# A gated sum of attention and a Fourier layer: the gate leaves VectorE's DFT updates for GpSimd's output stage

## The chip, the cores and the metric

The kernel runs on one core of a Trainium2 chip. A core has a matrix engine (TensorE, PE in the profile; its weight loads are listed as PEld), a vector engine (VectorE, DVE), a scalar engine (ScalarE, ACT), a general engine (GpSimd, POOL) and an engine that here only issues DMAs (SyncE, SP). Each engine executes its own instructions in order and waits on semaphores for the others. GpSimd also issues DMAs here, and these stand in its queue between its computations. The metric is the device time of one execution in microseconds (us), lower is better.

## The reference, cut to what matters

All matrices are f32. `x` is 2048 by 640. The two heavy branches are attention with 32 heads of 20 columns, and a Fourier layer written as products with DFT matrices. A sigmoid gate, one number per row of `x`, mixes the two.

```python
x = A_x
g = sigmoid((x * gate_w).sum(-1, keepdims=True))     # one gate per row
a = attention(x, wqkv) @ wo                           # 32 heads of 20 columns, softmax
re = x @ dft_hid_re.T ; im = x @ dft_hid_im.T
b = dft_seq_re @ re - dft_seq_im @ im                 # real part of the 2-D DFT
return g * a + (1 - g) * b
```

The question of this case is where the factor `1 - g` is applied to `b`, and by which engine.

## The kernel before

**Stages.** First come the projections of `x` (queries, keys, values, and part of the product with the hidden-dimension DFT). Then comes one long loop of 1024 steps over the attention: in each step PE multiplies keys and queries twice, ACT takes the exponential, and PE also makes, 41 steps ahead, the scores whose row maximum VectorE takes (`s_mm`, line 151 for the matmul, line 153 for the maximum). Every fourth step ends a cycle: PE multiplies the exponentials with the values in one block of 16 matmuls (`av_step`, line 435). Between the attention's matmuls PE gets the DFT's matmuls as fillers (`fill`): first the rest of the hidden-dimension products (`hid_tile`), and from about 600 us on the products along the sequence (`dft_step`, line 510). Last comes an output stage of 16 row tiles, in which PE multiplies the attention's result with `wo`.

**PSUM buffers.** The scores and the exponentials' inputs share five PSUM tiles, taken in turn (`bank`). A score tile is free again when VectorE has taken its maximum, so PE can run only some tiles ahead of VectorE. The output stage takes its PSUM tiles from the same five.

**The DFT along the sequence.** It is a block method with seven products (`PRODUCTS`) over halves of the rows and columns, so that each product's result is added to, or subtracted from, one, two or three quarter blocks of the result `y`. One unit is one product for one tile of 128 rows: 16 steps of DFT matmuls, 56 units in all. GpSimd prepares both operands: it combines the DFT matrix halves (line 406), and splits each operand into a rounded value and a rest (lines 94 and 95; tiles `part` for the DFT matrix, `a` for the data). `part` has three buffers.

**The end of a unit.** PE's two partial sums lie in PSUM. ACT copies one into the SBUF tile `m` (line 529), VectorE adds the other (line 530). Then `finish_y` runs once for each target, 96 times in all: it multiplies `m` with `1 - g` (or with its negative, from two small tiles `ngate`), and either writes that into the target tile `yt` (line 544, the first time) or adds the target's earlier content, which was loaded from DRAM (line 542). Three steps later SP stores `yt` to the scratch `y_scr` in DRAM. `run_extras` calls these pieces at the end of every fourth step, so the VectorE instructions of `finish_y` stand in the stretch in which PE executes its block of 16 matmuls.

**The output stage.** SP loads whole rows of `y` (`load_y`, tiles of 128 by 640 in buffers of `p`) and of the attention's result (`load_o`), ACT and VectorE split the latter (`fins`), PE makes two halves of a row tile with 15 matmuls each, and VectorE forms `g * ps + y` (line 701) and so frees the PSUM tile. The last attention unit's normalisation is spread into the same stage: its pieces (`rest`) put DMAs and one multiplication into GpSimd's queue, and the attention rows from tile 8 on can only be loaded after it.

```python
for fn in rest[:2]:      # GpSimd: store_l (4 DMAs), load_l (1 DMA)
    fn()
fins[1]()
for tt in range(NS):
    ...                  # PE; VectorE line 701, twice
    for fn in {2: rest[2:5], 3: rest[5:6], 4: rest[6:]}.get(tt, ()):
        fn()             # tt 2: reciprocal (VectorE), store_r, load_r; 3: norm; 4: store_o
```

Of the kernel before, what the change touches and what calls it, by code (L numbers as in the profile page):

```python
# [10 lines left out]
F32 = mybir.dt.float32  # L11
R = mybir.dt.float32r
AF = mybir.ActivationFunctionType
ALU = mybir.AluOpType
# [4 lines left out]
P = 128  # L19
# [5 lines left out]
NS = S // P  # L25
# [30 lines left out]
def mix_kernel(ctx: ExitStack, tc: tile.TileContext, xa, wqk, wb, cdft, wo, out):  # L56
    nc = tc.nc
    pe, act, dve, pool, sp = nc.tensor, nc.scalar, nc.vector, nc.gpsimd, nc.sync
    ctx.enter_context(tc.manual_schedule())

    def pools(**kw):
        return ctx.enter_context(tc.tile_pool(**kw))

    const = pools(name="const", bufs=1)
# [20 lines left out]
        pool.memset(f32(t), 1.0)  # L85
    logit = const.tile([P, NS], F32, name="logit")
    gate = const.tile([P, NS], F32, name="gate")
    ngate = {g: const.tile([P, NS], F32, name=f"ngate{g + 1}") for g in (1, -1)}

    def split(dst1, dst2, src, e1, e2):  # L90
        if e1 is act:
# [5 lines left out]
    def three(ps, st1, st2, mv1, mv2, first, last):  # L97
        pe.matmul(ps, st1, mv1, start=first, stop=False)  # L98
        pe.matmul(ps, st1, mv2, start=False, stop=False)  # L99
        pe.matmul(ps, st2, mv1, start=False, stop=last)  # L100
# [3 lines left out]
    def bank():  # L104
        return ps_w.tile([P, 512], F32, name=f"ps{next(turn) % 5}")
# [31 lines left out]
    def at_step(i, fn):  # L137
        later.setdefault(i, []).append(fn)
# [100 lines left out]
    def flush(keep=0):  # L239
        while len(stores) > keep:  # L240
            sp.dma_start(*stores.pop(0))
# [118 lines left out]
    for n, c in enumerate(order):  # L360
        for t in range(4):
            m = 4 * n + t
# [12 lines left out]
    act.activation(gate, logit, AF.Exp, scale=-1.0)  # L375
    dve.tensor_scalar(gate, gate, 1.0, None, op0=ALU.add)
    dve.reciprocal(gate, gate)
    for g in (1, -1):
        dve.tensor_scalar(ngate[g], gate, float(-g), float(g), op0=ALU.mult, op1=ALU.add)


    at = {}
# [106 lines left out]
    def dft_step(g):  # L489
# [34 lines left out]
        if s == NS - 1:  # L524
            m = apool[0].tile([P, HE], F32, name="m", bufs=2)
            y0, y1 = yp[0][:, :HE], yp[1][:, :HE]

            def read():
                act.activation(m, y0, AF.Copy)
                dve.tensor_tensor(m, y1, m, op=ALU.add)  # L530

            extras.append((now[0], read))
            for out_, y in zip(PRODUCTS[n][2], outs.pop((n, t))):
                extras.append((now[0] + 1, functools.partial(finish_y, out_, t, m, y)))
        yield

    def finish_y(target, t, m, y):
        sg, th, hf = target
        tt = th * HT + t
        gs = ngate[sg][:, tt : tt + 1]  # L540
        if (tt, hf) in seen:
            dve.scalar_tensor_tensor(y, m, gs, y, op0=ALU.mult, op1=ALU.add)
        else:
            dve.tensor_scalar(y, m, gs, None, op0=ALU.mult)
        seen.add((tt, hf))
        at_step(now[0] + 3, functools.partial(sp.dma_start, y_scr[tt, :, hf * HE : (hf + 1) * HE], y))

# [26 lines left out]
    def load_o(tt):  # L574
        raw = raw_tile()[:, : ND * P].rearrange("p (d c) -> p d c", d=ND)
        sp.dma_start(raw, o_scr[:, tt * P : (tt + 1) * P].rearrange("(d p) c -> p d c", p=P))

        def finish():
            o = part_tile().rearrange("p z c -> p (z c)")[:, : 2 * ND * P].rearrange("p (z d c) -> p z d c", z=2, d=ND)
            split(o[:, 0], o[:, 1], raw, act, dve)  # L580
            ops[tt] = o

        return finish
# [33 lines left out]
    for i in range(total + 1):  # L617
# [50 lines left out]
        if total - 10 <= i < total - 4 and i % 2 == 0:  # L668
            tt = (i - total + 10) // 2
# [11 lines left out]
    ys = {}  # L681

    def load_y(tt):
        ys[tt] = pair_tile().rearrange("p z c -> p (z c)")[:, :D]
        sp.dma_start(ys[tt], y_scr[tt])

    flush()
    for tt in range(4):
        load_y(tt)
    for fn in rest[:2]:  # L690
        fn()
    fins[1]()
    for tt in range(NS):
        y, o = ys.pop(tt), ops.pop(tt)
        for hf in range(2):
            ps = bank()[:, :HE]
            for d in range(ND):
                w = wos[d, hf]
                three(ps, o[:, 0, d], o[:, 1, d], w[:, 0], w[:, 1], d == 0, d == ND - 1)
            ye = y[:, hf * HE : (hf + 1) * HE]  # L700
            dve.scalar_tensor_tensor(ye, ps, gate[:, tt : tt + 1], ye, op0=ALU.mult, op1=ALU.add)  # L701
        if 0 < tt < NS - 3:
            load_y(tt + 3)
        for fn in {2: rest[2:5], 3: rest[5:6], 4: rest[6:]}.get(tt, ()):
            fn()
        if tt + 3 < NS:
            fins[tt + 3] = load_o(tt + 3)
        sp.dma_start(out[tt * P : (tt + 1) * P, :], y)
        if tt + 2 < NS:
            fins[tt + 2]()  # L710


# [33 lines left out]
```

## Time and profile before

| | |
|---|---|
| median of 3 runs | 2012.11 us (2010.03 to 2013.65) |
| profiled execution, its own time | 2012.72 us |
| its span in the profile | 2011.0 us |
| mean granted PE clock in it | 0.997 of full speed |
| busy: PE, DVE, ACT, POOL | 98%, 75%, 62%, 49% of the span |

The span runs from the first to the last instruction; 1.7 us of the execution's own time lie around it. A busy share is an average over stages. PE's matmuls are pipelined and their ends are modelled, so that a short stall can be hidden in "busy". In the timeline, a number in brackets is the idle time of the engine ahead of the instruction, with what ended it.

### The profile page before, as it was taken

How to read it: one execution, taken by the hardware profiler on the slowest of the kernel's cores; microseconds unless marked ns; L12 is line 12 of the kernel's file. 1: busy time of each engine (PE TensorE's matmuls, PEld its weight loads, DVE VectorE, ACT ScalarE, POOL GpSimd, SP SyncE). 2: the span in 40 equal slices, each digit the busy share in tenths (PEclk: the TensorE clock that was granted, in tenths of full speed). 3: DMA queues.
4: the chain of work that ended last, by engine and by line, in shares of the span. 5: the costliest groups of instructions: out<-in, count | busy, mean ns of one | idle time of the engine just before them, and what ended most of it. 6: DMA issues, size and time to landing. Idle time of an engine off the chain costs nothing. (4 is left out here: it accounts for less than half of the span.)

```text
span 2011.0 us, 44080 instructions
## 1 busy us (share of the span) xinstructions
PE 1974.8 (98%) x17080; PEld 1397.7 (70%) x17080; DVE 1501.9 (75%) x2516; ACT 1253.3 (62%) x2337; POOL 986.6 (49%) x898
## 2 busy tenths in 40 slices
PE   8999999999999999999999999999999999999999
PEld 7987767666675666666666666666666666666679
DVE  3144568878887888888888888888888888888423
ACT  4221147777776666677666666766766676667751
POOL 1210001111006888556368876974775689576510
PEclk9999999999999999999999999999999999999999
DMA  6653321313125475435266736563555556444345
GB/s 218 168 166 132 128 90 45 83 50 82 35 60 161 143 204 159 118 100 153 93 169 194 207 133 194 175 184 100 165 149 145 163 171 200 131 149 144 95 150 184
DMA packets 196514, 281.05 MB, mean 140 GB/s; under 512 B 73372, under 2 KB 137916, under 8 KB 194384
## 3 DMA queue, kind: packets, MB, share of 16 engines
q1 hardware_dynamic: 158992, 246.20, 39.6%
q0 software_dynamic: 37312, 32.03, 6.4%
q8 instruction: 134, 2.20, 0.5%
q14 instruction: 76, 0.62, 0.1%
HBM read 213.81 MB, written 63.70 MB: 138 GB/s over the span
## 5 line engine op out<-in xcount | busy, mean ns | idle before, releaser
L153 DVE TENSOR_REDUCE mx<-ps 128x1 f32<-128x512 f32 x2048 | 1262.2, 683 | 233.8 <-PE ps L151 230.1
L641 ACT ACTIVATE p<-ps 128x512 f32<-128x512 f32 x2048 | 1122.6, 598 | 446.0 <-PE ps L151 354.6
L151 PE MATMUL ps<-kst,qst 60*128 60x512 f32 x2048 | 926.1, 460 | 8.0 <-ACT p L641 3.7
L638 PE MATMUL ps<-qst,kst 62*128 62x512 f32 x2048 | 823.9, 409 | 9.0 <-DVE mx L153 7.6
L510 PE MATMUL yp<-a,part 64*128 64x320 f32 x5376 | 734.0, 309 | 0.1
L510 PEld LDWEIGHTS yp<-a,part 64*128 64x128 f32 x5376 | 596.6, 187 | 23.9 <-DVE m L530 0.3
L638 PEld LDWEIGHTS ps<-qst,kst 62*128 62x128 f32 x2048 | 376.9, 185 | 235.9 <-DVE mx L153 66.9
L435 PE MATMUL av<-p,v 128*21 128x512 f32 x4096 | 494.7, 599 | 0.1
L151 PEld LDWEIGHTS ps<-kst,qst 60*128 60x128 f32 x2048 | 372.0, 184 | 59.5 <-ACT p L641 27.7
L95 POOL TENSOR_TENSOR part<-raw,part 128x1024 fp32r<-128x1024 f32 x112 | 267.1, 2385 | 9.0
L435 PEld LDWEIGHTS av<-p,v 128*21 128x21 f32 x4096 | 98.8, 100 | 226.8 <-issue 219.8
L287 PE MATMUL yp<-wb,xs 64*128 64x320 f32 x1920 | 238.1, 308 | 0.4 <-ACT raw L295 0.3
L94 POOL CAST part<-raw 128x1024 fp32r<-128x1024 f32 x112 | 116.8, 1043 | 205.2 <-PE yp L510 198.6
L406 POOL TENSOR_TENSOR raw<-raw,raw 128x1024 f32<-128x1024 f32 x78 | 188.3, 2414 | 50.1 <-DMA raw<-in_cdft 39.6
L287 PEld LDWEIGHTS yp<-wb,xs 64*128 64x128 f32 x1920 | 205.7, 187 | 9.1 <-ACT raw L295 0.6
L467 POOL TENSOR_TENSOR o<-o,rb 128x512 f32<-128x512 f32 x32 | 41.6, 1300 | 160.7 <-DMA rb<-r_scr 130.0
L94 POOL CAST wb<-raw 128x966 fp32r<-128x966 f32 (+1 forms) x4 | 3.4, 856 | 229.7 <-PE av L435 195.5
L95 POOL TENSOR_TENSOR a<-araw,a 128x320 fp32r<-128x320 f32 x112 | 98.1, 876 | 9.0
L95 DVE TENSOR_TENSOR p<-ps,p 128x512 fp32r<-128x512 f32 x40 | 27.5, 691 | 94.2 <-ACT p L92 94.2
L98 PE MATMUL ps<-xs,part 128*128 128x512 f32 x200 | 80.7, 403 | 9.1 <-ACT xs L92 7.5
L92 ACT ACTIVATE p<-ps 128x512 fp32r<-128x512 f32 x40 | 23.7, 597 | 101.5 <-PE ps L100 101.5
L420 POOL TENSOR_TENSOR araw<-araw 128x320 f32<-128x320 f32 x80 | 71.4, 892 | 20.4 <-DMA araw<-a_scr 19.9
(67 smaller groups left out, 1339.0 us busy)
## 6 DMA issues: line engine op xcount, KB each, us to landing
raw<-in_cdft SPq DMA_DIRECT2D x192, 512.0 KB
araw<-a_scr SPq DMA_DIRECT2D x192, 160.0 KB
qk_scr<-p SPq DMA_DIRECT2D x40, 512.0 KB
y_scr<-yt SPq DMA_DIRECT2D x96, 160.0 KB
kst<-qk_scr POOLq DMA_DIRECT2D x32, 320.0 KB, 12.2
qst<-qk_scr POOLq DMA_DIRECT2D x64, 160.0 KB, 8.8
a_scr<-raw SPq DMA_DIRECT2D x64, 160.0 KB
yt<-y_scr SPq DMA_DIRECT2D x64, 160.0 KB
```

The lines of the kernel that those rows point to most:

```text
L94: e1.tensor_copy(dst1, src)
L95: e2.tensor_tensor(dst2, src, f32(dst1), op=ALU.subtract)
L98: pe.matmul(ps, st1, mv1, start=first, stop=False)
L151: pe.matmul(ps, q[b : b + KROWS, qt * P : (qt + 1) * P], k[b : b + KROWS, kc * 512 : (kc + 1) * 512], start=True, stop=True)
L153: return lambda: dve.tensor_reduce(mx[n][:, h, qt, kc : kc + 1], ps, axis=AX.X, op=ALU.max)
L287: pe.matmul(yp[h][:, :HE], xs[r, xz, d, cs], w[r, wz, d, :HE], start=d == 0 and z == 0, stop=d == ND - 1 and z == 2)
L406: pool.tensor_tensor(raws[0], raws[0], raws[1], op=ALU.add if PRODUCTS[n][0][1][0] > 0 else ALU.subtract)
L420: pool.tensor_tensor(raws[0], raws[0], raws[1], op=ALU.add if PRODUCTS[n][1][1][0] > 0 else ALU.subtract)
L435: pe.matmul(av[32 * j : 32 * j + DH + 1, :], v[:, kt, h * (DH + 1) : (h + 1) * (DH + 1)], pp[qc][:, h, :], start=kt == 0, stop=kt == NS - 1)
L510: pe.matmul(yp[h][:, :HE], c[r, cz, cs], a[r, az], start=s == 0 and z == 0, stop=s == NS - 1 and z == 2)
L638: pe.matmul(pt, k[b : b + KROWS + 2, kt * P : (kt + 1) * P], q[b : b + KROWS + 2, qc * 512 : (qc + 1) * 512], start=True, stop=True)
L641: act.activation(pp[:, h], pt, AF.Exp, scale=float(DH) ** -0.5)
```

## The change

`finish_y` no longer multiplies with the gate and no longer runs on VectorE. GpSimd adds `m` to the target or subtracts it, or, the first time, writes `m` times plus or minus one. So `y_scr` holds `b` without its factor. In the output stage GpSimd multiplies each loaded row tile of `y`, 128 by 640, with `1 - g` in place (`scale_y`). Tiles 0 and 1 are multiplied ahead of the loop, tile `tt + 2` at the end of turn `tt`, so two turns ahead of its use. In GpSimd's queue the first multiplication stands directly behind `load_l`, those of tiles 2 and 3 before `store_r`, that of tile 4 between `load_r` and `norm`, that of tile 5 between `norm` and `store_o`, and the rest behind `store_o`. The order on PE, ACT and SP stays as it was.

```diff
-    ngate = {g: const.tile([P, NS], F32, name=f"ngate{g + 1}") for g in (1, -1)}
+    ngate = const.tile([P, NS], F32, name="ngate")
...
-    for g in (1, -1):
-        dve.tensor_scalar(ngate[g], gate, float(-g), float(g), op0=ALU.mult, op1=ALU.add)
+    dve.tensor_scalar(ngate, gate, -1.0, 1.0, op0=ALU.mult, op1=ALU.add)
...
     def finish_y(target, t, m, y):
         sg, th, hf = target
         tt = th * HT + t
-        gs = ngate[sg][:, tt : tt + 1]
         if (tt, hf) in seen:
-            dve.scalar_tensor_tensor(y, m, gs, y, op0=ALU.mult, op1=ALU.add)
+            pool.tensor_tensor(y, y, m, op=ALU.add if sg > 0 else ALU.subtract)
         else:
-            dve.tensor_scalar(y, m, gs, None, op0=ALU.mult)
+            pool.tensor_scalar(y, m, float(sg), None, op0=ALU.mult)
         seen.add((tt, hf))
...
+    def scale_y(tt):
+        pool.tensor_scalar(ys[tt], ys[tt], ngate[:, tt : tt + 1], None, op0=ALU.mult)
+
     flush()
     for tt in range(4):
         load_y(tt)
     for fn in rest[:2]:
         fn()
     fins[1]()
+    for tt in range(2):
+        scale_y(tt)
     for tt in range(NS):
...
         sp.dma_start(out[tt * P : (tt + 1) * P, :], y)
         if tt + 2 < NS:
+            scale_y(tt + 2)
             fins[tt + 2]()
```

## The prediction

> **What bounds the kernel now.** I read the page first, then the groups by line, then the stage of the DFT products alone, then single cycles in the timeline, and last the output stage. The page and the groups:
>
> ```profile
> span 2011.0 us, 44080 instructions
> PE 1974.8 (98%) x17080; PEld 1397.7 (70%) x17080; DVE 1501.9 (75%) x2516; ACT 1253.3 (62%) x2337; POOL 986.6 (49%) x898
> ...
> L638 PE MATMUL ps<-qst,kst 62*128 62x512 f32 x2048 | 823.9, 409 | 9.0 <-DVE mx L153 7.6 <-DVE p L95 0.7 <-ACT p L641 0.3
> ```
>
> PE is the bound; the other engines matter only where PE waits for them. The one wait with a DVE name on it is 7.6 us in front of line 638, ended by row maxima. The first row of the next fence is the stretch in which `finish_y` runs; its PE idle time is 1265.00 - 1256.75 = 8.25 us.
>
> ```profile
> 670.00:1935.00 1265.00, 1256.75 (x11534) 843.92 (x11532) 1039.44 (x1740) 884.82 (x1653) 870.36 (x742) 1.00 0.51 152
> 1060.00:1320.00 260.00, 255.76 (x2337) 171.85 (x2335) 225.50 (x369) 178.82 (x332) 212.41 (x182) 1.00 0.59 178
> ```
>
> The columns are length, then busy time and count of PE, PEld, DVE, ACT, POOL, then clock and DMA. More than half of the idle time, 260.00 - 255.76 = 4.24 us, lies in the 260 us in which POOL is 82% busy (212.41). Why there, three durations tell (min/median/max in ns, from the view of tile `m`), and one cycle in the timeline (start, duration):
>
> ```profile
> L542 DVE SCALAR_TENSOR_TENSOR yt<-m,ngate,yt x64: 529/550/2671, 865.2 to 1934.1; 128x320 f32<-128x320 f32 x64
> L530 DVE TENSOR_TENSOR m<-yp,m x56: 468/492/493, 673.8 to 1931.2; 128x320 f32<-128x320 f32 x56
> L544 DVE TENSOR_SCALAR yt<-m,ngate x32: 366/412/2531, 680.0 to 1210.9; 128x320 f32<-128x320 f32 x32
> ```
>
> ```profile
> 1306.72 0.14 PEld L435 LDWEIGHTS av<-p,v 128*21 128x21 f32 x8 [0.29 <-issue]
> 1307.47 3.65 DVE L542 SCALAR_TENSOR_TENSOR yt<-m,ngate,yt 128x320 f32<-128x320 f32 x2
> 1308.13 2.63 POOL L406 TENSOR_TENSOR raw<-raw,raw 128x1024 f32<-128x1024 f32 x1
> 1308.55 2.92 SPq L621 DMA_DIRECT2D y_scr<-yt  x2
> ...
> 1311.04 2.47 DVE L153 TENSOR_REDUCE mx<-ps 128x1 f32<-128x512 f32 x4
> 1311.77 0.50 PE L638 MATMUL ps<-qst,kst 62*128 62x512 f32 x1 [1.18 <-DVE mx L153]
> ...
> 1315.02 0.28 PE L179 MATMUL ps<-ident,nm 128*16 128x128 f32 x1
> 1315.22 0.14 PEld L435 LDWEIGHTS av<-p,v 128*21 128x21 f32 x8
> ```
>
> Two updates that take 0.55 us each when nothing is in their way took 3.65 us, and the second ended 0.36 us after a POOL instruction of 2.63 us (1308.13 + 2.63 = 1310.76; 1307.47 + 3.65 = 1311.12). Line 530, which has one operand in PSUM, never took over 493 ns beside the same POOL. So the updates, which read and write SBUF alone, are held by a running POOL instruction, the row maxima start late, the five PSUM tiles stay full, and PE stands 1.18 us. A cycle without that, between two starts of PE's block of 16, against 8.50 us above:
>
> ```profile
> 1005.58 0.14 PEld L435 LDWEIGHTS av<-p,v 128*21 128x21 f32 x8 [0.28 <-issue]
> 1012.18 0.14 PEld L435 LDWEIGHTS av<-p,v 128*21 128x21 f32 x8 [0.28 <-issue]
> ```
>
> That is 6.60 us with the same number of DFT fillers. The held cycle also has the small transpose of line 179 (0.28), so the hold cost 8.50 - 6.60 - 0.28 = 1.62 us where the idle column shows 1.18, 1.37 times as much.
>
> **The change part by part.** (1) *The updates leave DVE.* 96 instructions go, and with them the holds. Line 153 reads PSUM, and no other DVE instruction of this stage has two large SBUF operands. At least PE's 7.6 us named after DVE come back; at most the whole idle time, 8.25, times 1.37, so 11.3 us. I take the middle, 9.5. What is late next in a released cycle is PE itself, as in the 6.60 us cycle.
>
> (2) *The updates come to POOL*, 64 as an add of two tiles and 32 as a multiplication by a constant. The nearest rows are POOL's own, same tile size, and the larger forms:
>
> ```profile
> L95 POOL TENSOR_TENSOR a<-araw,a 128x320 fp32r<-128x320 f32 x112 | 98.1, 876 | 9.0
> L94 POOL CAST a<-araw 128x320 fp32r<-128x320 f32 x112 | 52.7, 471 | 25.4 <-DMA araw<-a_scr 20.3
> L467 POOL TENSOR_TENSOR o<-o,rb 128x512 f32<-128x512 f32 x32 | 41.6, 1300 | 160.7 <-DMA rb<-r_scr 130.0 <-ACT p L641 29.5 <-DMA yt<-y_scr 1.3
> L95 POOL TENSOR_TENSOR part<-raw,part 128x1024 fp32r<-128x1024 f32 x112 | 267.1, 2385 | 9.0
> L94 POOL CAST part<-raw 128x1024 fp32r<-128x1024 f32 x112 | 116.8, 1043 | 205.2 <-PE yp L510 198.6 <-PE ps L638 1.8 <-PE ps L151 1.4
> ```
>
> 64 x 0.88 + 32 x 0.47 = 71 us (87 us if the multiplication costs as much as an add). POOL has 1265.00 - 870.36 = 395 us free in the stretch. Each update now also waits in POOL's queue for line 530 of its unit; behind it stand the next splits of `part` and `a` for PE, and the DMAs that load `kst` and `qst`. What covers that is POOL's lead: the last row says that 198.6 of the 205.2 us that it stood before a split ended when PE gave back a `part` buffer, so POOL is normally early by most of a buffer's life. I take nothing for it; uncovered, it costs PE up to two updates, 1.8 us, a unit. SP's store of `yt`, three steps later, waits for POOL instead of DVE; in the held cycle above it waited 2.92 us for DVE, so SP loses nothing.
>
> (3) *The output stage gets 16 multiplications of 128 by 640 on POOL.* The trace has no such instruction. With one input, the casts (471 at 320 columns, 1043 at 1024) give 0.73 us; as costly as an add (1300 at 512, 2385 at 1024) it would be 1.57. I take 0.85, near the cast, as one tensor is read. What counts is its place:
>
> ```profile
> 1937.25 2.00 POOL L451 DMA_DIRECT2D l_scr<-o  x4 [28.85 <-ACT o L442]
> 1944.00 0.58 POOL L454 DMA_DIRECT2D lc<-l_scr  x1 [4.74 <-DVE p L701]
> ...
> 1961.49 1.31 POOL L467 TENSOR_TENSOR o<-o,rb 128x512 f32<-128x512 f32 x1 [4.62 <-DMA rb<-r_scr]
> 1963.10 2.04 POOL L475 DMA_DIRECT2D o_scr<-o  x4 [0.29 <-POOL o L467]
> ```
>
> ```profile
> 1936.27 0.35 PE ps L98
> ```
>
> ```profile
> 1938.71 0.55 DVE L701 SCALAR_TENSOR_TENSOR p<-ps,gate,p 128x320 f32<-128x320 f32 x1 [0.21 <-PE ps L100]
> 1940.91 0.55 DVE L701 SCALAR_TENSOR_TENSOR p<-ps,gate,p 128x320 f32<-128x320 f32 x1 [1.65 <-PE ps L100]
> 1941.38 0.81 DVE L95 TENSOR_TENSOR part<-raw,part 128x640 fp32r<-128x640 f32 x1
> ...
> 1969.86 0.83 DVE L95 TENSOR_TENSOR part<-raw,part 128x640 fp32r<-128x640 f32 x1 [2.00 <-ACT part L92]
> ```
>
> POOL issues its four stores at 1937.25 and then stands until 1944.00, when the load of what they wrote may go; the wait is put down to DVE, but it fits the stores' landing. The first multiplication is queued behind that load: 1944.58 + 0.85 = 1945.43, where line 701 for tile 0 ran at 1938.71. DVE waits there, and behind it stands the split of tile 2 (line 95, before at 1941.38). DVE now does line 701 twice (1945.50, 1945.97), arrives at the split at 1946.44, finds POOL in the multiplication of tile 2 until 1947.15, and is done at 1947.97. PE needs it in its third matmul for tile 2. Tiles take 4.40 us (two halves of 1940.91 - 1938.71 = 2.20), so tile 2 starts at 1936.27 + 8.80 = 1945.07, the third matmul 2 x 2.20 / 15 = 0.29 later, at 1945.36. **PE stands 2.6 us** here. The cheap end (0.73, no hold by POOL) gives 1.8, the dear one (1.57, held for one whole multiplication) 4.2. PSUM has room: tile 0's two halves are freed before the sixth half needs one.
>
> Further on, the whole chain shifts with PE, except that the multiplication of tile 4 stands before `norm` (hidden in its 4.62 us wait) and that of tile 5 before the store of `o`, which shifts by 0.85. The split of tile 8 ended at 1969.86 + 0.83 = 1970.69 and was due at 1936.27 + 8 x 4.40 + 0.29 = 1971.76: 1.07 us of room, enough for 0.85; at 1.57 plus a hold of 1.57 it would cost 2.1. Later multiplications have two turns, 8.8 us, and cost nothing.
>
> Here a rule speaks against the change. The split of the output stage took 0.81 us while POOL was idle. The Trainium skill, GPSIMD Engine Reference, § 1 Specifications, says that GpSimd's SBUF interfaces are shared with VectorE and that instructions with two SBUF inputs or in a 2-port mode contend. Lines 542 and 530 agree: 2671 against 493 ns at most. By this rule the splits of this stage, two SBUF inputs each, are open to holds for the first time, which is what the 0.71 us above is.
>
> **The sum.** -9.5 + 2.6 = -6.9 us. Against the profiled execution's own 2012.72 us that is 2005.8; that execution was 0.6 above the median of 2012.11, so the median after is **2005.2 us**. With the ends: -11.3 + 1.8 = -9.5, so 2002.6; and -7.6 + 4.2 + 2.1 = -1.3, so 2010.8. A difference under 0.2%, 4.0 us, can hardly be told from none here, so that the dear output stage would read as no change.
>
> **The rivals.** *A dear multiplication on POOL.* If a multiplication by a column of 128 numbers runs like an add or worse, the output stage gives back 5 to 9 us and the kernel stands at 2008.2 to 2012. For it: no such row in the trace. Against it: one tensor input, as in the cast.
>
> *PE does not gain.* Another wait takes the place of the holds, and only the output stage's price is left: 2012.1 + 2.6 = 2014.7, within 0.2%. Against it: the 7.6 us in the groups, and the undisturbed cycle of 6.60.
>
> *POOL becomes the bound, and the kernel is slower.* In 1060 to 1320 POOL has 260.00 - 212.41 = 47.6 us free. Line 530 ran 56 times between 673.8 and 1931.2, so a unit lasts 1257.4 / 55 = 22.9 us; with two targets each (all products but the last two) some 22 updates fall into these 260 us. From 47.6 / 22 = 2.2 us each, waits for line 530 included, POOL falls behind and PE waits for `part`. At 2.8 us each this costs 22 x 0.6 = 13 us: 2012.1 - 9.5 + 2.6 + 13 = 2018.2. For it: one update in POOL's strict order now holds back everything behind it until PE has finished a unit. Against it: 0.88 us, and POOL's lead. The Trainium skill, GPSIMD Engine Reference, § 4.1 Engine selection, advises against this: elementwise work on two inputs belongs on VectorE, as GpSimd is about twice as slow. The rows agree on the engine's time, 876 against 550 ns; by engine time alone the change would lose, but neither engine is the bound.
>
> **How the numbers follow.** Forecast (below 2008.1): 0.73. Dear multiplication: 0.10, and no gain: 0.06, both within 0.2%, so 0.16. POOL the bound, or a like starvation through the `qst` loads behind the updates: 0.11, slower. The range for 8 in 10 is the forecast's with its ends, 2002.6 to 2010.8, which takes in most of the dear case and leaves out about 0.2.
>
> **What would show it.** Right: no idle time of PE before line 638 ended by line 153 beyond about 1 us; cycles with an update as long as those without; PE idle time of 670 to 1935 under 2 us; the updates on POOL at about 0.9 and 0.5 us; in the output stage the first line 701 at about 7 us after its place before, and one PE stall of 2 to 3 us at tile 2. Wrong: PE waits for `part`, `a` or `qst`; a second stall at tile 8; multiplications over 1.6 us; or holds that remain without the updates.

## The result, and the profile after

| | median | range | ratio to before, 95% interval |
|---|---|---|---|
| before, same series | 2012.88 us | 2010.03 to 2014.97 | |
| changed kernel | **2001.86 us** | 2000.50 to 2004.27 | 0.995, 0.9936 to 0.9965 |
| changed kernel, second series | 2001.94 us | 1997.65 to 2004.88 | 0.9948, 0.993 to 0.9966 |
| changed kernel, third series | 2001.13 us | 1998.0 to 2004.21 | 0.9944, 0.993 to 0.9958 |

The kernel is faster by 0.5%, 11 us by the medians. The forecast was 6.9 us less, 2005.2 us; the measured median lies 0.7 us below the lower end of its range, 2002.6. Each ratio weighs the executions of both kernels in its own series, not the medians, and leaves out one of the kernel before in the second series, 2287.46 us at a granted clock of 0.753. The profiled execution took 2004.27 us, the slowest of its four, so that the two profiles differ by 8.5 us only; what follows compares stages, not ends. The page of the changed kernel, its group for line 636 (638 before), and the two stretches that were shown of before:

```profile
span 2002.5 us, 44148 instructions
...
PE 1972.5 (99%) x17080; PEld 1402.0 (70%) x17080; DVE 1428.3 (71%) x2419; ACT 1253.5 (63%) x2337; POOL 1096.9 (55%) x1010
...
L636 PE MATMUL ps<-qst,kst 62*128 62x512 f32 x2048 | 818.9, 407 | 2.1 <-DVE mx L153 0.9
```

```profile
670.00:1935.00 1265.00, 1261.83 (x11586) 853.29 (x11584) 966.57 (x1646) 885.67 (x1655) 956.38 (x845) 1.00 0.52 153
1060.00:1320.00 260.00, 259.58 (x2381) 174.58 (x2373) 207.07 (x353) 180.56 (x339) 231.91 (x205) 1.00 0.61 182
```

PE's wait for row maxima went from 7.6 to 0.9 us, and in 1060 to 1320 us, where POOL is now busy for 89% of the time, PE stands 0.42 us instead of 4.24. The first row also has PE's stall in the output stage in it, as that stage now begins 12 us earlier: 1.55 of its 3.17 us of idle time, which leaves 1.6. The cycle that was held before (8.50 us) looks like this now (timeline: start, duration):

```profile
1297.17 1.70 POOL L540 TENSOR_TENSOR yt<-yt,m 128x320 f32<-128x320 f32 x2
1298.24 0.14 PEld L434 LDWEIGHTS av<-p,v 128*21 128x21 f32 x8 [0.27 <-issue]
1299.08 1.14 SPq L619 DMA_DIRECT2D y_scr<-yt  x2
1300.65 2.49 DVE L153 TENSOR_REDUCE mx<-ps 128x1 f32<-128x512 f32 x4 [1.58 <-PE ps L151]
1305.03 0.14 PEld L434 LDWEIGHTS av<-p,v 128*21 128x21 f32 x8
```

From block to block it takes 1305.03 - 1298.24 = 6.79 us, 1.71 less. The two updates begin on POOL 1.07 us before the block and are done 0.63 us into it (1297.17 + 1.70 = 1298.87); VectorE waits for PE (1.58 us), no longer PE for VectorE; SP's stores take 1.14 us where they took 2.92. Over the whole stretch from the first update to the last regular cycle, the distances between these blocks add up to 1248.81 us against 1259.84, 11.0 less, nearly all of it gained in eleven of the cycles in which an update had been held. In the two other traces of the changed kernel they add up to 1248.51 and 1248.85 us.

POOL's new instructions (min/median/max in ns from the view by line, and the group of the output stage's multiplications):

```profile
L540 POOL TENSOR_TENSOR yt<-yt,m x64: 858/871/897, 855.7 to 1919.6; 128x320 f32<-128x320 f32 x64
L542 POOL TENSOR_SCALAR yt<-m x32: 998/1011/1038, 673.3 to 1198.1; 128x320 f32<-128x320 f32 x32
L686 POOL TENSOR_SCALAR p<-p,ngate 128x640 f32<-128x640 f32 x16 | 30.1, 1886 | 10.9 <-DMA p<-y_scr 8.1 <-DVE p L704 1.8 <-DVE part L95 0.8
```

The output stage, with line 704 in the place of 701:

```profile
1924.08 0.42 PE L98 MATMUL ps<-a,part 128*128 128x320 f32 x1
1930.71 0.57 POOL L453 DMA_DIRECT2D lc<-l_scr  x1 [3.58 <-DMA l_scr<-o]
1931.32 7.47 POOL L686 TENSOR_SCALAR p<-p,ngate 128x640 f32<-128x640 f32 x4
1933.25 1.01 DVE L704 SCALAR_TENSOR_TENSOR p<-ps,gate,p 128x320 f32<-128x320 f32 x2 [6.88 <-POOL p L686]
1934.18 0.81 DVE L95 TENSOR_TENSOR part<-raw,part 128x640 fp32r<-128x640 f32 x1
1935.05 0.42 PE L100 MATMUL ps<-a,part 128*128 128x320 f32 x1 [1.60 <-DVE part L95]
1961.87 0.41 PE L98 MATMUL ps<-a,part 128*128 128x320 f32 x1 [0.45 <-ACT part L92]
1962.73 0.42 PE L100 MATMUL ps<-a,part 128*128 128x320 f32 x1 [0.30 <-DVE part L95]
1997.94 0.55 DVE L704 SCALAR_TENSOR_TENSOR p<-ps,gate,p 128x320 f32<-128x320 f32 x1 [1.59 <-PE ps L100]
```

VectorE stands 6.88 us for the first scaled tile, PE then 1.60 us for the split of tile 2, and again around tile 8. The stage lasts 1998.49 - 1924.08 = 74.4 us, against 2007.46 - 1936.20 = 71.3 before (the first row of the next fence is from the timeline of the kernel before):

```profile
1936.20 0.42 PE L98 MATMUL ps<-a,part 128*128 128x320 f32 x1
...
2006.91 0.55 DVE L701 SCALAR_TENSOR_TENSOR p<-ps,gate,p 128x320 f32<-128x320 f32 x1 [1.65 <-PE ps L100]
```

So: 11.0 us gained in the DFT products, 3.2 lost in the output stage. This loss is not a fixed size: in the two other traces of the changed kernel the stage lasts 73.1 and 74.1 us, so that 1.9 and 2.8 are lost. The start of the loop and its first cycles, which the change doesn't touch, made up for most of the rest in this pair (first block 2.2 us earlier, the cycles until the first update 1.1 longer); up to the block ahead of the first update it took 672.8 us before, and 668.4, 671.7 and 673.1 us in the three traces of the changed kernel.

### The profile page after: what moved, and what is told of

Read it like the earlier page. It is cut to its first block, busy times and chain, and to the rows that moved or that the text cites. A ratio compares the mean times of both kernels' runs of the same rounds, so it can differ in the third digit from the quotient of the medians.

```text
span 2002.5 us, 44148 instructions
## 1 busy us (share of the span) xinstructions
PE 1972.5 (99%) x17080; PEld 1402.0 (70%) x17080; DVE 1428.3 (71%) x2419; ACT 1253.5 (63%) x2337; POOL 1096.9 (55%) x1010
## 5 line engine op out<-in xcount | busy, mean ns | idle before, releaser
L94 POOL CAST part<-raw 128x1024 fp32r<-128x1024 f32 x112 | 116.2, 1038 | 109.0 <-PE yp L509 104.4
L540 POOL TENSOR_TENSOR yt<-yt,m 128x320 f32<-128x320 f32 x64 | 55.1, 873 | 84.4 <-DVE m L529 82.4
```

The source lines that it names most:

```text
L94: e1.tensor_copy(dst1, src)
L540: pool.tensor_tensor(y, y, m, op=ALU.add if sg > 0 else ALU.subtract)
```

## The experiments

Theory 1 was the prediction's: VectorE's updates are held while POOL works, and the holds stall PE. Theory 2: VectorE simply had too much to do between PE's blocks. The first four runs tell these apart; three more take the output stage apart, and one puts the updates back on VectorE; the last two compare the best version once more.

**The changed kernel again.** 

> The changed kernel once more, as the base for the next three. Both theories: 2001.9 us, 0.995 of before. It also says how far the median of the changed kernel moves between series; the first series gave 2000.5 to 2004.3.

Measured: 2001.94 us, ratio 0.9948 (0.993 to 0.9966). It repeats.

**VectorE's time back, without a second SBUF input.**

```diff
             pool.tensor_scalar(y, m, float(sg), None, op0=ALU.mult)
+        dve.tensor_reduce(spare[:, :1], m, axis=AX.X, op=ALU.max)
```

> The changed kernel, and each of the 96 updates also puts one maximum over m (128 by 320, one SBUF input) into VectorE's queue at the place where the update was; its result is not used. Theory 1 (VectorE's updates cost time because an instruction with two SBUF inputs is held by a running GpSimd instruction): about 0.45 us each, 43 us more of VectorE, but no holds, so no change against the changed kernel, 2002 us, and PE's idle time ahead of line 636 ended by row maxima stays near 1 us. Theory 2 (VectorE simply had 83 us less to do in the stretches between PE's blocks): half of the gain or more is lost, 2007 us or above.

**The same place, with two SBUF inputs.**

```diff
             pool.tensor_scalar(y, m, float(sg), None, op0=ALU.mult)
+        dve.tensor_tensor(spare, m, m, op=ALU.add)
```

> As the run before, but the added VectorE instruction is an add of m and m into a spare tile (two SBUF inputs, 128 by 320), again unused. Theory 1: it is held like the updates were, up to 2.6 us, and most of the gain is lost, 2009 to 2013 us, with PE idle 5 to 8 us ahead of line 636. Theory 2: as long as the maximum, so the same time as that run, 2007 us.

Measured: 2002.87 us with the maximum (ratio 0.9956, 0.9939 to 0.9973), 2024.93 us with the add (1.0073, 1.0051 to 1.0096). The added instructions by line, and line 638, first with the maximum, then with the add:

```profile
L544 DVE TENSOR_REDUCE spare<-m x96: 462/476/489, 674.4 to 1917.8; 128x1 f32<-128x320 f32 x96
```

```profile
L638 PE MATMUL ps<-qst,kst 62*128 62x512 f32 x2048 | 818.4, 406 | 2.1 <-DVE mx L153 0.9 <-DVE p L95 0.7 <-ACT p L641 0.3
```

```profile
L544 DVE TENSOR_TENSOR spare<-m x96: 468/926/6068, 681.6 to 1951.3; 128x320 f32<-128x320 f32 x96
```

```profile
L638 PE MATMUL ps<-qst,kst 62*128 62x512 f32 x2048 | 828.5, 411 | 16.5 <-DVE mx L153 14.8 <-DVE p L95 0.7 <-ACT p L641 0.3
```

Both add an instruction of about 0.47 us when undisturbed. The one with one SBUF input is never longer than 489 ns and costs nothing that these runs can tell; 46 us of VectorE's time are free. The one with two is held up to 6.07 us, and PE waits 14.8 us for row maxima (its profile is of the slowest of six executions, 2032.27 us). Theory 2 falls. That the add writes 320 columns and the maximum one is not the difference: line 530 writes 320 too, with one input in PSUM, and never took over 493 ns. The add costs more than the updates had cost (the expectation was 2009 to 2013), and it was held more often: 63 of the 96 adds took over 0.12 us more than the shortest, of the 96 updates before 44. That this is because it comes at the moment at which POOL begins the updates is likely, but not shown by a run.

**Before, with short POOL instructions.**

```diff
+        if e1 is pool and src.shape[-1] == 1024:
+            for k in range(0, 1024, 256):
+                pool.tensor_tensor(dst2[:, k : k + 256], src[:, k : k + 256], f32(dst1)[:, k : k + 256], op=ALU.subtract)
+            return
         e2.tensor_tensor(dst2, src, f32(dst1), op=ALU.subtract)
```

The combination in `load_c` is cut in the same way; the updates stay on VectorE with the gate.

> The kernel before, with its updates on VectorE, but GpSimd's instructions on two tiles of 128 by 1024 (subtraction and combination for part) are cut into four of 128 by 256, so that none of them lasts much over 0.75 us. GpSimd gets about 110 us more work in all. Theory 1 (a hold lasts until the running GpSimd instruction ends): no update over about 1.6 us, PE's stalls nearly gone, 2003 to 2006 us. Theory 2: VectorE's work is the same, so 2013 us or more.

Measured: 2005.42 us, ratio 0.9966 (0.9953 to 0.9979). The updates' adds and line 644, which is 638 of before:

```profile
L548 DVE SCALAR_TENSOR_TENSOR yt<-m,ngate,yt x64: 531/663/2534, 863.5 to 1926.7; 128x320 f32<-128x320 f32 x64
```

```profile
L644 PE MATMUL ps<-qst,kst 62*128 62x512 f32 x2048 | 824.7, 409 | 2.7 <-DVE mx L157 1.5 <-DVE p L99 0.8 <-ACT p L647 0.3
```

With VectorE's instructions untouched and more work on POOL (busy 1070.7 us, before 986.6), PE's wait falls from 7.6 to 1.5 us and the time by 0.34%: it is the length of POOL's instructions that counted. One update still took 2.53 us, against the expected 1.6 at most; see the last section.

**The output stage without the multiplications.** The edit leaves `scale_y` empty, so the output lacks the factor `1 - g`; the run serves only to measure the stage.

> The changed kernel without its 16 multiplications by one minus the gate (the output is left without that factor). It shows what the output stage pays. By the trace of the changed kernel: PE's stalls there (1.9 us at tile 2, 1.4 us around tile 8) go, so 3.2 us less than the changed kernel, 1998.7 us. Rival (the multiplications are covered, the stalls come from elsewhere): 2001.9 us.

Measured: 1998.98 us, 0.9926 (0.9914 to 0.9939). The stage lasts 71.3 us again.

**The multiplications on ScalarE.**

```diff
-        pool.tensor_scalar(ys[tt], ys[tt], ngate[:, tt : tt + 1], None, op0=ALU.mult)
+        act.activation(ys[tt], ys[tt], AF.Copy, scale=ngate[:, tt : tt + 1])
```

> The changed kernel with the same 16 multiplications on ScalarE, which is busy 14.5 of the last 82 us. If the price is GpSimd's queue and its 1.89 us for each: both stalls go, as in the run without multiplications, 1998.7 us; ScalarE takes about 0.74 us for each. Rival (the price is the wait of VectorE for a scaled tile, whoever makes it): 2001.9 us. This is also the version that would beat both kernels.

Measured: 1997.80 us, 0.9923 (0.991 to 0.9936). Its group, and the first and last instruction of the stage:

```profile
L686 ACT ACTIVATE p<-p,ngate 128x640 f32<-128x640 f32 x16 | 13.0, 828 | 25.8 <-DMA p<-y_scr 25.8
```

```profile
1920.48 0.41 PE L98 MATMUL ps<-a,part 128*128 128x320 f32 x1
...
1991.18 0.55 DVE L704 SCALAR_TENSOR_TENSOR p<-ps,gate,p 128x320 f32<-128x320 f32 x1 [1.65 <-PE ps L100]
```

1991.73 - 1920.48 = 71.25 us, as before the change: the price was POOL's, not the wait for a scaled tile as such.

**Another place in POOL's queue.** `scale_y(0)` and `scale_y(1)` stand ahead of `rest[:2]`.

> The changed kernel with the multiplications of tiles 0 and 1 ahead of the store and the load of the last attention unit's sums in GpSimd's queue, not behind them. If the stall at tile 2 is the place in the queue: it goes (1.9 us), the sums' chain starts about 2.6 us later but gains back PE's stall, so that the stall around tile 8 stays between 1 and 2.5 us: 1999.5 to 2001 us. Rival (it is only the length of the multiplications): the stall at tile 2 stays, 2001.9 us.

Measured: 1999.32 us, 0.9935 (0.9923 to 0.9947), and the stall at tile 2 is gone:

```profile
1921.87 3.99 POOL L686 TENSOR_SCALAR p<-p,ngate 128x640 f32<-128x640 f32 x2 [3.65 <-DMA p<-y_scr]
1925.81 2.06 POOL L450 DMA_DIRECT2D l_scr<-o  x4
```

```profile
1924.38 0.55 DVE L704 SCALAR_TENSOR_TENSOR p<-ps,gate,p 128x320 f32<-128x320 f32 x1 [0.28 <-PE ps L100]
```

VectorE waits for PE (0.28 us) where it waited 6.88 for POOL. The stage lasts 71.65 us, 0.4 over before, less than the 1 to 2.5 us expected around tile 8, and the time is just under the expected 1999.5 to 2001.

**The updates back on VectorE, the multiplications on POOL.** In `finish_y`, `pool` becomes `dve`; all else as changed.

> Half of the change alone: the updates are back on VectorE, but without the gate (an add of two SBUF tiles, or a multiplication by a constant), and GpSimd multiplies in the output stage. Theory 1 (two SBUF inputs, or the 2-port mode of the multiplication, are held): the holds are all back, and the output stage's 3.2 us come on top, 2013 to 2016 us beside 2010 to 2013 of before. Rival (it was the gate's column as a scalar operand that made the updates long): the holds are gone, 2002 to 2005 us.

Measured: 2016.08 us (2006.44 to 2020.43), ratio 1.0018 (1.0004 to 1.0033). The updates by line:

```profile
L540 DVE TENSOR_TENSOR yt<-yt,m x64: 468/485/2634, 855.6 to 1924.0; 128x320 f32<-128x320 f32 x64
L542 DVE TENSOR_SCALAR yt<-m x32: 304/318/2519, 672.6 to 1201.6; 128x320 f32<-128x320 f32 x32
```

The time is at the upper end of the 2013 to 2016 expected for theory 1. The holds are back without the gate's column, up to 2.6 us, so the gate as an operand was not their cause; and the half of the change that remains costs about 0.2%. The profiled execution was the fastest of twelve (2006.44). The times of kernels with holds spread by up to 14 us here, those without by 4 to 7. Holds that fall differently in each execution would explain that, but each run has one trace, and the kernels with the widest spread were also executed more often, so it is not shown.

**ScalarE's version beside the changed kernel.** 

> The changed kernel once more, on the same chip as the next run: 2002 us, 0.995 of before. It decides whether the version with ScalarE's multiplications is faster than the changed kernel, which the two earlier series could only tell by ratios that overlap.

> The version with the 16 multiplications on ScalarE once more: 1998 to 1999 us, 3 to 4 us less than the changed kernel in the same series, with an output stage as long as before the change (71.25 us against 73 to 74.4). Rival (the gap between the two series was the chips'): 2002 us.

Measured: 2001.13 us (0.9944, 0.993 to 0.9958) and 2000.52 us (0.9934, 0.9919 to 0.9949). The expected 1998 to 1999 us did not come, and in this series the two cannot be told apart by their times. In the traces the output stage lasts 74.1 us in the one and 71.25 in the other. ScalarE's version beats the kernel before in both series; that it beats the changed kernel is shown for its stage, and for the whole only by ratios whose intervals overlap.

## Why the prediction was right, point by point

**The cause.** Right, and shown from both sides: VectorE's time with a maximum of one SBUF input costs nothing, with an add of two it costs more than was gained; and before gets faster when POOL's instructions get shorter. Only the prediction's description of what is held, instructions that "read and write SBUF alone", was too wide: the maximum does that too, and was never held. One input does not protect by itself either, as VectorE's multiplication by a constant, with one SBUF input and 320 columns written to SBUF, was held up to 2.52 us (line 542 above).

**The size of the gain.** 9.5 us were taken, the middle of 7.6 and 11.3; the cycles gave 11.0. The factor of 1.37 between idle time and lost time, worked out from one cycle, was the better guide than the idle time itself. This term accounts for 1.5 of the missing 4 us; the factor comes from a single cycle, so that its good fit may be luck.

**The updates on POOL.** The adds took 0.87 us as taken. The multiplications by plus or minus one took 1.01, not 0.47: slower than the adds, though they read one tile. The sum came to 55.1 + 32.2 = 87.3 us, not 71; the prediction's own dear figure, 87, was misadded, as 96 x 0.88 is 84.5. It was covered: no wait of PE for `part` or `a` came up, and its one wait for a `qst` load (1.95 us, at 628 us) lies ahead of the first update. POOL's wait for a `part` buffer, 198.6 us before, is 104.4 now, and that is where the lead went:

```profile
POOL part L94 <- PE yp L509: 104.4, 26, 9.2
```

**The output stage.** 2.6 us were taken, 3.2 came, but by other terms. The multiplication was sized at 0.85 with 1.57 as the dear end, and took 1.89: the step that failed is "near the cast, as one tensor is read". By luck two errors went the other way. The load behind which it stands left 6.63 us after the stage began (1930.71 - 1924.08), not 7.7; and the split of tile 2 was not held at all (0.81 us, while POOL was in four multiplications on end), where 0.71 us of hold were taken; it began 0.98 us into a multiplication, and the last section shows why that matters. So PE lost 1.9 us at tile 2 (1.60 of them as idle time) instead of 2.6, and 1.3 around tile 8, where the forecast took nothing and its dear end 2.1. The wait ahead of that load was read rightly: it is now named as the stores' landing. The stall around tile 8 was within its bounds (0 to 2.1).

**The range and the rivals.** The sum of the two profiles' stages is -7.9 us (-11.03 + 3.15), near the forecast; the medians say -11, and the interval of the ratio reaches from -7 to -13 us. So both terms lay within their bounds, and the median still fell 0.7 us below the range. The start, which moved by 4.6 us among the three traces of the changed kernel, had no term in the sum. Whether the remainder lies there, or in holds that fall differently in each execution of the kernel before, stays open, as that kernel has one trace. The dear multiplication came true without its consequence; the times given for it, 2008.2 to 2012, start from the profiled execution, and from the median they are 2007.6 to 2011.6. Two of the prediction's signs of being wrong came, a second stall at tile 8 and multiplications over 1.6 us, and together they cost less than the gain. POOL did not become the bound at 89%, and the longer engine time of an update on POOL (0.87 against 0.55 us) decided nothing.

## What to carry to other kernels

An engine that is off the critical path can still stall it by holding the instructions of a third: look for instructions whose maximum is several times their median, and see what the neighbour was doing at that moment. A move to a slower engine pays where it ends such collisions and the new engine has a lead; but follow the in-order queue that it joins, since a cheap instruction behind a DMA wait is late by that wait. For the second half, an idle engine with no such wait (here ScalarE) was the better home by the length of its stage, 71.25 us against 73.1 to 74.4.

## What the runs showed of the hardware that was not expected

**A hold can span several POOL instructions, but seldom does.** In the kernel with short POOL instructions an update was held by two in a row (VectorE, then POOL, from the timelines):

```profile
1050.09 2.53 DVE L548 SCALAR_TENSOR_TENSOR yt<-m,ngate,yt 128x320 f32<-128x320 f32 x1
```

```profile
1050.15 1.30 POOL L473 TENSOR_TENSOR o<-o,rb 128x512 f32<-128x512 f32 x1
1051.38 0.88 POOL L426 TENSOR_TENSOR araw<-araw 128x320 f32<-128x320 f32 x1
1052.33 0.61 POOL L94 CAST a<-araw 128x320 fp32r<-128x320 f32 x1
```

The second began before the first had ended (1050.15 + 1.30 = 1051.45), and the update ended 0.36 us after the second (1052.26). Such an overlap alone does not prolong a hold: in the four kernels with updates or adds on VectorE, 198 of these were held by over 0.12 us, and 189 of them ended 0.18 to 0.36 us after the end of a POOL add or cast, in 53 cases although POOL's next computation had already begun. Six times a hold ran on past the end of a POOL computation, each time into an instruction that had already begun; what sets these apart stays open. So cutting an instruction helped also where the pieces follow without a gap.

The add that was held for 6.07 us met a chain of two adds, three DMA issues and a combination. Most DMA issues do not hold: of 30 updates and adds that began beside DMA issues alone, 22 took at most 25 ns over the shortest of their kind. The other eight took 0.2 to 0.8 us longer; why, no run tells.

**POOL's multiplication holds only in its first part.** In the changed kernel's output stage nine splits, with two SBUF inputs each, started while POOL was in a multiplication of 1.89 us. Six of them started 0.98 us or more after it and took 0.81 to 0.83 us, as long as with POOL idle. The other three started 0.41 to 0.56 us after it and took 0.91 to 1.06. One of them (VectorE, then POOL):

```profile
1976.41 1.06 DVE L95 TENSOR_TENSOR part<-raw,part 128x640 fp32r<-128x640 f32 x1
```

```profile
1976.00 1.89 POOL L686 TENSOR_SCALAR p<-p,ngate 128x640 f32<-128x640 f32 x1 [0.77 <-DMA p<-y_scr]
```

All three ended 1.47 us after the multiplication's start (here 1976.41 + 1.06 - 1976.00), and so, to 0.03 us, did the 13 others that were held in the six more traces with these multiplications on POOL. The longest, in the run with the multiplications first, took 1.51 us. As a split alone takes 0.82, the multiplication lets it through about 0.65 us after its start, an estimate from these two numbers, where adds and casts on POOL held to near their own end. It goes the other way too: in that run a multiplication that began 0.16 us after a split took 2.41 us. The multiplication is also the slower one for each element (1886 / 640 = 2.9 ns, an add of 320 columns 2.7, a cast of 1024 columns 1.0). The Trainium skill, GPSIMD Engine Reference, § 4.1 Engine selection, calls GpSimd's work on one input roughly line-rate. The cast agrees with that, the multiplications of this case do not, and for them the measurement stands.
